# Top-k attention followed by a PReLU MLP: where a unit's first sign, k's copy, the weight preparation and the first loads of v stand

## The chip, the cores and the metric

The kernel runs on one core of a Trainium2 chip. The metric is the device time of one execution in microseconds (us). TensorE is called PE here, its weight loads PEld, VectorE DVE, ScalarE ACT, GpSimd POOL and SyncE SP. Each engine takes its own instructions in order; engines wait for each other through semaphores. A transfer (DMA) is issued from the instruction queue of SP, ACT or POOL and then runs on 16 shared DMA engines.

## The reference

64 heads (8 batches of 8) of 576 rows and 64 columns go through attention that keeps the 32 largest scores of each row; the heads of a batch are put side by side (4608 rows of 512), and a two-layer MLP with a PReLU between follows.

```python
scores = scale * np.matmul(q, k.transpose(0, 1, 3, 2))
kth = np.partition(scores, -32, axis=-1)[..., -32:-31]
scores = np.where(scores >= kth, scores, -1000000000.0)
attn = softmax(scores)
x = np.matmul(attn, v)            # then (b, s, h*d)
h = x @ w_in
g = np.maximum(h, 0.0) + alpha * np.minimum(h, 0.0)
out = g @ w_out
```

## The kernel before

**Tiles, units, pairs.** Two heads make a pair; a pair is cut into nine tiles of 128 rows by 576 scores (the ninth takes the last 64 rows of both heads). There are 32 pairs and 288 tiles. A program loop walks over the tiles; one turn is called a tick. Two tiles in a row make a unit (`unit_of`), the ninth tile of a pair a unit of one, so that a pair is 2+2+2+2+1. Every instruction is recorded in the order in which this loop names it, engine by engine: nothing is reordered later.

**One tile.** PE forms the scores (`scores`, L327, into `ps`). ACT copies them with a per-row shift into `b` (`act_b`, L336), takes their signs into `h` with a count per row (`act_s`, L342, the count is read out by a second instruction), and their exponentials into `e` (`act_e`, L347, once a unit). POOL turns the count into a flip word `SG` (`side_of`, L352). DVE flips the tile into `y` (L358), takes the largest eight of five strides (L369), merges them (L383, L385), picks the limit, and masks (`mk`, L432) a tile that is seven ticks old. POOL multiplies mask and exponentials into `w` (L442), SP transposes `w` by a DMA into `wT` (L455), PE multiplies with v (`av`, L493, into `pu`), DVE takes the reciprocal of the row sums (`rz`, L510), ACT scales into `xb` (L522).

**ACT's order in a unit.** In a unit's first tick ACT stands in this order: evacuations of the MLP step of the tick before, `b`, `b`, what the calendar of that tick holds, the sign of the first tile. In the second tick: evacuations of the first tick's MLP step, the sign of the second tile, the calendar, `e`.

**Preparing a pair.** `prep_plan` lists steps with ticks relative to a pair's base: transposes of q (`pe_q`, L196), copy of q (`act_q`, L199) and transposes of k (`pe_k`, L207), copy of k (`act_k`, L211) and transposes of the last 64 rows (`pe_t`, L215), their copy, then moments: `GK` (L228), `pr` (L237), `P` (`dve_p`, L245), `st`, and a short chain on DVE (L270 `sq` to L287) that gives the shift `NT` for `b`. `pq`, `pk`, `pt` share one PSUM bank, so each waits for the copy of the one ahead of it. `act_v` (L202) casts v from a float32 stage into `v_bf`.

**The MLP.** `mlp_steps` gives steps, one taken per tick from the queue `back`: 4 matmuls into `ph` (L696), evacuated by ACT with Relu into `gT` (L702), or 6 to 7 matmuls into `pz` (L710, L714), evacuated into `o_sb` (L719). A step's evacuation is run at the start of the next tick (queue `after`). In the main part there is one PSUM bank for it (`ps_m`), so a step's first matmul waits for the evacuation of the step before.

**Weights.** The first 48 ticks take steps of `weight_steps` instead: load alpha, load `w_out` in 16 blocks through three stage buffers, scale each twice on ACT (L643 by 1-alpha into `w_out_b`, L644 by alpha into `xT`, which is still free), load `w_in` with a cast from POOL (L631, two transfers for each of four blocks, at ticks 3, 7, 11, 15), transpose each block whole by a DMA from SP (L635, `w_inT`), and multiply (`w_id`).

Of the kernel before, what the change touches and what calls it, by code (L numbers as in the profile page):

```python
# [9 lines left out]
FP32 = mybir.dt.float32  # L10
# [6 lines left out]
S = 576  # L17
# [14 lines left out]
def kernel(  # L32
# [83 lines left out]
    def early_sets():  # L116
        for i in range(2):
            nc.gpsimd.memset(ksts[i][:, :, 0:1], 1.0)
            nc.gpsimd.memset(ksts[i][:, :, 129:130], 1.0)
            nc.gpsimd.memset(ksts[i][64:128, 4, :], 0.0)  # L120
        for t_ in st_vs:
            nc.vector.memset(t_[64:128, 4, :], 0.0)
            nc.vector.memset(t_[0:64, 5, :], 0.0)
        for t_ in v_bfs:
            nc.vector.memset(t_[:, :, D:V1], 1.0)
            nc.vector.memset(t_[64:128, 4, D:V1], 0.0)
            nc.vector.memset(t_[0:64, 5, D:V1], 0.0)
        for i in range(KW):
            nc.vector.memset(iota[:, i:i + 1], (1.0 + 2 * i) ** 2)

# [14 lines left out]

    def load_v(p):
        hA = 2 * p
        st_v = st_vs[p % 2]
        nc.sync.dma_start(st_v[:, 0:4, :], vf[hA, 0:512, :].rearrange("(c p) d -> p c d", p=128))
        nc.sync.dma_start(st_v[0:64, 4, :], vf[hA, 512:S, :])  # L150
        nc.sync.dma_start(st_v[64:128, 5, :], vf[hA + 1, 0:64, :])
        nc.sync.dma_start(st_v[:, 6:10, :],
                          vf[hA + 1, 64:S, :].rearrange("(c p) d -> p c d", p=128))

    ORDER = [divmod(n, TPP) for n in range(N0)]
    LAST = range(P0, NPAIR)
# [17 lines left out]
    def prep_plan(p):  # L174
# [33 lines left out]
                                    ident_f)  # L208

        def act_k():  # L210
            nc.scalar.copy(d["qkT"][:, 1, 0:512], d["pk"])  # L211

        def pe_t():
            d["pt"] = bank("pt", [128, 2, 64])
# [73 lines left out]
                                    ALU.bitwise_xor, ALU.bitwise_or)  # L288

        if p == 1:  # L290
            ts = [-9, -8, -7, -6, -5, -4, -3, -2, -2, -2, -2, -2, -1, -1, 1]
# [3 lines left out]
        steps = [dict(pe=[pe_q]), dict(act=[act_q], pe=[pe_k]), dict(act=[act_k], pe=[pe_t]),  # L295
                 dict(act=[act_t], pe=[pe_g]), dict(act=[act_g], pe=[pe_r]),
                 dict(dve=[dve_p]), dict(pe=[pe_s]), dict(act=[act_m]), dict(dve=[dve_2]),
                 {dvx: [dve_3]}, dict(dve=[dve_4]), {dvx: [dve_4b]}, dict(dve=[dve_5]),
                 dict(dve=[dve_6]), dict(act=[act_v])]
        if p == 0:  # L300
            ts = [-16, -15, -14, -13, -12] + [-11] * 6 + [-2]
            steps = [dict(pe=[pe_q, pe_g, pe_t]), dict(act=[act_q, act_g, act_t], pe=[pe_r, pe_k]),
                     dict(dve=[dve_p]), dict(act=[act_k], pe=[pe_s]), dict(act=[act_m])] + steps[8:]
        return list(zip(ts, steps))

    tiles = {}
# [33 lines left out]
    def act_s(n):  # L340
        h = attn.tile([128, S], BF16, name="h", bufs=1)
        nc.scalar.activation(h, tiles[n]["b"], AF.Sign, accum_out=S_all[:, n:n + 1])  # L342
# [250 lines left out]
    def last_pz():  # L593
        o0 = t7 + 384
        for h, (pool, tag) in enumerate(((ps_a, "pa"), (ps_m, "misc"))):
# [9 lines left out]
            (nc.scalar.copy if h == 0 else nc.vector.tensor_copy)(o_sb[:, 0:256], pz)  # L605
            nc.sync.dma_start(out[o0:o0 + 128, cs], o_sb[:, 0:256])

    def weight_steps():
        hold = {}

        def alpha():
            a16 = mlp.tile([128, DM], FP32, name="a16", tag="stage", bufs=3)[0:NFT, 0:128]
            nc.sync.dma_start(a16, moe_alpha.rearrange("(t p) -> t p", p=128))
            hold["a16"] = a16

        def alpha1():
            aps = ps_m.tile([128, NFT], FP32, name="aps", tag="misc")
            nc.tensor.transpose(aps, hold["a16"], ident_f[0:NFT, 0:NFT])
            hold["aps"] = aps
            hold["inT"] = mlp.tile([128, NKT, NFT, 128], BF16, name="w_inT", tag="gT", bufs=1)  # L620

        def alpha2():
            nc.scalar.copy(alpha_sb, hold["aps"])
            nc.gpsimd.tensor_scalar(alpha1m, alpha_sb, -1.0, 1.0, ALU.mult, ALU.add)

        def lin(f):
            return xT[:, f // 4, DM * (f % 4):DM * (f % 4 + 1)]

        def w_in(kk):
            for hf in range(0, DFF, 1024):  # L630
                nc.gpsimd.dma_start(w_in_b[:, kk, hf:hf + 1024],  # L631
                                    moe_w_in[kk * 128:(kk + 1) * 128, hf:hf + 1024])

        def w_in2(kk):
            nc.sync.dma_start_transpose(hold["inT"][:, kk, :, :], w_in_b[:, kk, :])  # L635

        def w_out(f):
            hold[f] = mlp.tile([128, DM], FP32, name="w_stage2", tag="stage", bufs=3)
            nc.sync.dma_start(hold[f], moe_w_out[f * 128:(f + 1) * 128, :])

        def w_out2(f):
            ws = hold.pop(f)
            nc.scalar.activation(w_out_b[:, f, :], ws, AF.Copy, scale=alpha1m[:, f:f + 1])  # L643
            nc.scalar.activation(lin(f), ws, AF.Copy, scale=alpha_sb[:, f:f + 1])  # L644

        done = [0]

        def w_id(kk, lim):
            if done[0] == 0:
                hold["pl", kk] = ps_m.tile([128, DM], FP32, name="pl", tag="misc")  # L650
            for f in range(done[0], lim):
                nc.tensor.matmul(hold["pl", kk], hold["inT"][:, kk, f, :], lin(f),
                                 start=(f == 0), stop=(f == NFT - 1))
            done[0] = lim % NFT

        def w_id2(kk):
            nc.scalar.copy(w_id_b[:, kk, :], hold["pl", kk])

        yield alpha, None
        yield (lambda: None), None  # L660
        yield (lambda: (alpha1(), w_out(0), w_out(1))), alpha2
        for f in range(NFT):
            yield ((lambda f=f: (w_out(f + 2) if f + 2 < NFT else None,
                                 w_in(f // 2) if f < 8 and f % 2 == 0 else None)),
                   (lambda f=f: w_out2(f)))
            yield ((lambda f=f: w_id(0, min(done[0] + 2, f)) if f >= 6 else None),
                   (lambda f=f: w_in2(f // 2) if f < 8 and f % 2 == 1 else None))
        yield (lambda: w_id(0, NFT)), (lambda: w_id2(0))
        for kk in range(1, NKT):
            for lim in (4, 8, 12, 16):  # L670
# [78 lines left out]
    with tc.manual_schedule(engines={E.PE, E.Activation, E.DVE, E.Pool, E.SP}):  # L749
# [66 lines left out]

        load(0, nc.scalar)
        load(1)
        plan(0)
        plan(1)  # L820
        early_sets()
        load_v(0)
        load_v(1)
        for t in range(-16, 0):
            for eng in ("act", "pool", "pe", "dve"):
                run(t, eng)
# [7 lines left out]
        n = 0  # L834
        end = max(NT + 24, 0)
        while n < end or back or after:
            for p in range(2, NPAIR):
                if n == max(0, BASE[p] - 18):
                    load(p)
                    plan(p)  # L840
                if n == max(0, BASE[p] - 13):
                    load_v(p)
# [5 lines left out]
            if n < NT:  # L848
                n0, m, i = unit_of[n]
                if i == 0:  # L850
                    act_b(n0)
                    if m == 2:
                        run(n, "act")
                    act_s(n)
                    if m == 1:
                        run(n, "act")
                        act_e(n0)
                else:
                    act_s(n)
                    run(n, "act")  # L860
                    act_e(n0)
# [6 lines left out]
            while back and credit > 0.0 and (first or nb == 2):  # L868
# [195 lines left out]
```

## Time and profile before

| | |
|---|---|
| Median of three runs | 873.18 us (868.11, 873.18, 873.46) |
| Profiled execution | 871.45 us; span of its instructions 869.6 us |
| PE busy | 714.7 us (82%) |
| POOL busy | 431.1 us (50%) |
| Mean granted clock of TensorE | 0.928 |
| Moved by DMA | 99.34 MB, mean 114 GB/s |

The page gives busy time by engine, the span in 40 slices, the chain of waits that ended last, and groups of equal instructions with the idle time ahead of them and what ended it. The span is 1.85 us shorter than the execution's own time. A tick lasts some 2.7 us, a pair some 25.

### The profile page before, as it was taken

To read this page: it belongs to the slowest core of one execution; us is meant where nothing else is said; L and a number is where in the kernel's file an instruction comes from. 1 tells how busy PE (TensorE), PEld (TensorE's weight loads), DVE (VectorE), ACT (ScalarE), POOL (GpSimd) and SP (SyncE) were. 2 spreads that over 40 slices of the span, in tenths; PEclk is the share of its full clock that TensorE was granted. 3 is DMA by queue.
4 is the path that set the end of the run, shared out by engine and by line. 5 is a ranking of instruction groups with operands and counts; after the bars stand their busy time and mean duration, and the time that the engine had idled before them with its cause. 6 is when DMAs were issued, how large, how long until landed. Compare 5 with 4: busy or idle time off the path is not lost. (4 is left out here: it accounts for less than half of the span.)

```text
span 869.6 us, 20320 instructions
## 1 busy us (share of the span) xinstructions
PE 714.7 (82%) x5697; PEld 424.1 (49%) x5771; DVE 814.2 (94%) x4900; ACT 789.5 (91%) x1873; POOL 431.1 (50%) x630
## 2 busy tenths in 40 slices
PE   6666778778977789877987789987897988899996
PEld 4333444434544445544454445643455554566575
DVE  4988999999999999999999999998999999988992
ACT  6989999989999999998999989999999899979871
POOL 1454555555455555554554555554555555545530
PEclk8567789899999999999998999989999999999999
DMA  7799645554675645464477556564365644535452
GB/s 159 157 159 209 128 92 102 121 94 88 134 153 111 105 108 124 99 134 88 110 159 121 88 104 119 118 132 97 84 125 123 124 100 85 100 74 100 89 99 56
DMA packets 342616, 99.34 MB, mean 114 GB/s; under 512 B 334672, under 2 KB 334944, under 8 KB 342496
## 3 DMA queue, kind: packets, MB, share of 16 engines
q1 hardware_dynamic: 340144, 95.58, 56.0%
q0 software_dynamic: 1152, 2.10, 1.8%
q8 instruction: 47, 0.77, 0.4%
q14 instruction: 73, 0.60, 0.2%
q10 hardware_dynamic: 1200, 0.30, 0.2%
HBM read 36.71 MB, written 9.44 MB: 53 GB/s over the span
## 5 line engine op out<-in xcount | busy, mean ns | idle before, releaser
L442 POOL TENSOR_TENSOR w<-mk,e 128x576 bf16<-128x576 bf16 x250 | 319.1, 1277 | 333.1 <-DVE mk L432 186.3
L369 DVE MAX8 C<-y 128x8 f32<-128x112 f32 (+1 forms) x1440 | 380.0, 264 | 0.1
L327 PE MATMUL ps<-qkT 64*128 64x288 f32 (+1 forms) x1280 | 252.8, 467 | 36.9 <-ACT b L336 36.5
L336 ACT ACTIVATE b<-ps,NT 128x576 f32<-128x576 f32 x288 | 202.4, 761 | 5.7 <-PE ps L327 5.7
L342 ACT ACTIVATE h<-b 128x576 bf16<-128x576 f32 x288 | 202.9, 705 | 1.6
L696 PE MATMUL ph<-xT,w_in_b 128*128 128x128 bf16 (+2 forms) x997 | 151.2, 293 | 41.6 <-ACT gT L702 38.4
L327 PEld LDWEIGHTS ps<-qkT 64*128 64x128 f32 (+1 forms) x1280 | 131.2, 190 | 97.7 <-ACT b L336 60.8
L347 ACT ACTIVATE e<-b 128x1152 bf16<-128x1152 f32 (+1 forms) x158 | 174.3, 1103 | 0.0
L358 DVE TENSOR_SCALAR y<-b,SG 128x576 int32<-128x576 int32 x288 | 147.4, 512 | 11.2 <-POOL SG L352 8.6
L383 DVE MAX8 L<-C 128x8 f32<-128x40 f32 x864 | 155.7, 180 | 0.1
L432 DVE TENSOR_SCALAR mk<-b,KP 128x576 bf16<-128x576 f32 x282 | 143.8, 510 | 0.0
L714 PE MATMUL pz<-w_out_b,gT 128*128 128x512 bf16 x543 | 132.4, 380 | 1.2 <-issue 0.5
L696 PEld LDWEIGHTS <-w_in_b 128*128 128x128 bf16 x1024 | 80.9, 100 | 105.8 <-issue 81.6
L702 ACT ACTIVATE gT<-ph 128x512 bf16<-128x512 f32 x140 | 85.9, 621 | 26.4 <-PE ph L696 26.2
L385 DVE MATCH_REPLACE8 C<-L,C 128x40 f32<-128x40 f32 x576 | 103.8, 180 | 0.0
L714 PEld LDWEIGHTS <-gT 128*128 128x128 bf16 x560 | 51.6, 98 | 68.5 <-issue 14.0
L493 PE MATMUL pu<-v_bf,wT 128*128 128x65 bf16 (+1 forms) x1600 | 69.1, 198 | 12.3 <-DMA wT<-w 11.1
L352 POOL TENSOR_SCALAR SG<-S_all 128x1 int32<-128x1 f32 x288 | 65.2, 227 | 22.0 <-ACT h L342 21.8
L493 PEld LDWEIGHTS <-wT 128*128 128x128 bf16 (+1 forms) x1600 | 64.9, 103 | 22.3 <-DMA wT<-w 11.7
L442 POOL TENSOR_TENSOR wm<-mk,e 128x576 bf16<-128x576 bf16 x32 | 40.9, 1277 | 49.0 <-DVE mk L432 46.4
L342 ACT ACTIVATION_READ_ACCUMULATOR h<-b 128x1 f32 x288 | 62.8, 218 | 0.0
L522 ACT ACTIVATE xb<-pu,rz 128x64 bf16<-128x64 f32 x224 | 54.6, 371 | 0.0
(113 smaller groups left out, 724.1 us busy)
## 6 DMA issues: line engine op xcount, KB each, us to landing
out_dram<-o_sb SPq DMA_DIRECT2D x34, 256.0 KB, 2.3
st_q<-in_q_dram SPq DMA_DIRECT2D x64, 128.0 KB, 2.8
st_v<-in_v_dram SPq DMA_DIRECT2D x64, 128.0 KB, 2.6
kst<-in_k_dram SPq DMA_DIRECT2D x62, 128.0 KB, 2.7
w_stage<-in_moe_w_out_dram SPq DMA_DIRECT2D x16, 256.0 KB, 3.3
w_in_b<-in_moe_w_in_dram POOLq DMA_DIRECT2D x8, 256.0 KB, 6.7
wT<-w SPq DMA_TRANSPOSE x128, 3.3
st_q<-in_q_dram SPq DMA_DIRECT2D x32, 32.0 KB, 2.5
```

The source lines that it names most:

```text
L327: nc.tensor.matmul(o_, l_, r_, start=True, stop=True)
L336: nc.scalar.activation(t["b"].rearrange("p (a c) -> p a c", a=2), t["ps"], AF.Identity, bias=NT0[:, p * TPP + j:p * TPP + j + 1], scale=ON ...
L342: nc.scalar.activation(h, tiles[n]["b"], AF.Sign, accum_out=S_all[:, n:n + 1])
L347: nc.scalar.activation(e, tiles[n0]["bu"], AF.Exp, scale=scl)
L358: nc.vector.tensor_scalar(t["y"].bitcast(I32), t["b"].bitcast(I32), FLIP, SG[:, n:n + 1], ALU.bitwise_xor, ALU.bitwise_xor)
L369: return [lambda g=g: nc.vector.max(out=C[:, n % TPP, g, :], in_=y[:, g:S // 8:NSEG, :]) for g in range(NSEG)]
L383: ops.append(lambda r=r, src=src: nc.vector.max(out=L[:, 8 * r:8 * r + 8], in_=src))
L432: nc.vector.tensor_scalar(t["mk"], t["b"], row_limit(n), None, ALU.is_ge)
L442: nc.gpsimd.tensor_tensor(dst, t["mk"], t["e"], ALU.mult)
L493: nc.tensor.matmul(o_, wT[:, 4 * side + c, cs], d["v"][:, 5 * side + c, :], start=(c == 0), stop=(c == 4))
L696: nc.tensor.matmul(hold[f][:, i, :], w_in_b[:, kk, (f + i) * 128:(f + i + 1) * 128], xT[:, kk, c0:c0 + tb], start=(kk == 0), stop=(kk == N ...
L714: nc.tensor.matmul(pz[0:m], hold["gT"][:, f, r0:r0 + m], w_out_b[:, f, :], start=False, stop=(f == NFT - 1))
```

## The change

- **Signs.** In a unit of two, both signs now stand in the second tick, behind the evacuations of the first tick's MLP step. Units of one keep their order.
- **k's copy.** `act_k` moves from the calendar of the next unit (behind its two `b`) to a new slot `actz` at the very end of the tick of `pe_k`, behind `e`. For pair 0 it goes to DVE.
- **v of pairs 0 and 1.** Loaded by casting transfers from POOL's queue straight into `v_bf`, with no stage and no `act_v`: pair 0 at the start, pair 1 one part at the end of each of ticks 8 to 11. The pad rows of all `v_bf` are now zeroed over their whole width by DVE.
- **Weights.** alpha is loaded right behind the loads of pairs 0 and 1. The five first scalings by 1-alpha go to POOL, one per tick in ticks 2 to 6, with the one by alpha on ACT; the other eleven blocks take one scaling per tick with a free tick behind most of them. The casts of `w_in` are issued at ticks 3, 11, 19, 27, and each transposition is cut into four, two ticks apart. The last three `w_id` take three steps instead of four. In all 49 steps instead of 48.

```diff
-            nc.vector.memset(t_[64:128, 4, D:V1], 0.0)
-            nc.vector.memset(t_[0:64, 5, D:V1], 0.0)
+            nc.vector.memset(t_[64:128, 4, :], 0.0)
+            nc.vector.memset(t_[0:64, 5, :], 0.0)
...
+    def load_v(p, parts=range(4)):
...
+        dst = v_bfs[p][:, :, 0:D] if p < 2 else st_vs[p % 2]
+        en = nc.gpsimd if p < 2 else nc.sync
...
+        for i in parts:
+            en.dma_start(*moves[i])
...
         def act_k():
-            nc.scalar.copy(d["qkT"][:, 1, 0:512], d["pk"])
+            (nc.vector.tensor_copy if p == 0 else nc.scalar.copy)(d["qkT"][:, 1, 0:512], d["pk"])
...
-        steps = [dict(pe=[pe_q]), dict(act=[act_q], pe=[pe_k]), dict(act=[act_k], pe=[pe_t]),
+        steps = [dict(pe=[pe_q]), dict(act=[act_q], pe=[pe_k], actz=[act_k]), dict(pe=[pe_t]),
...
-        def w_in2(kk):
-            nc.sync.dma_start_transpose(hold["inT"][:, kk, :, :], w_in_b[:, kk, :])
+        def w_in2(kk, i):
+            nc.sync.dma_start_transpose(wh["inT"][:, kk, 4 * i:4 * i + 4, :],
+                                        w_in_b[:, kk, 512 * i:512 * i + 512])
...
+        def scale(f, one_m, pool=False):
+            dst, s = (w_out_b[:, f, :], alpha1m) if one_m else (lin(f), alpha_sb)
+            if pool:
+                nc.gpsimd.tensor_scalar(dst, wh[f], s[:, f:f + 1], None, ALU.mult)
+            else:
+                nc.scalar.activation(dst, wh[f], AF.Copy, scale=s[:, f:f + 1])
...
+        ins = {3 + 8 * kk: (lambda kk=kk: w_in(kk)) for kk in range(NKT)}
+        more = {7 + 8 * kk + 2 * i: (lambda kk=kk, i=i: w_in2(kk, i))
+                for kk in range(NKT) for i in range(4)}
...
+        for f in range(5):
+            yield ((lambda f=f, k_=k_: (w_out(f + 2), scale(f, True, True), put_in(k_))),
+                   (lambda f=f: scale(f, False)))
+            k_ += 1
+        for f in range(5, NFT):
+            yield ((lambda f=f, k_=k_: (w_out(f + 2), put_in(k_))),
+                   (lambda f=f: scale(f, True)))
+            yield ((lambda f=f, k_=k_: (w_id(0, min(done[0] + 2, f) if k_ > 12 else 0),
+                                        put_in(k_ + 1))),
+                   (lambda f=f: scale(f, False)))
+            k_ += 2
+            if f % 6 != 4:
+                yield (lambda k_=k_: put_in(k_)), None
+                k_ += 1
...
+            if 8 <= n < 12:
+                put(n, "end", lambda i=n - 8: load_v(1, [i]))
...
                     act_b(n0)
                     if m == 2:
                         run(n, "act")
-                    act_s(n)
-                    if m == 1:
+                    else:
+                        act_s(n)
                         run(n, "act")
                         act_e(n0)
                 else:
+                    act_s(n0)
                     act_s(n)
...
             run(n, "pe")
+            run(n, "actz")
```

More of the change, by code (lines that the diff above doesn't have):

```diff
@@ L606, in last_pz, with load_alpha @@
             nc.sync.dma_start(out[o0:o0 + 128, cs], o_sb[:, 0:256])
-    def weight_steps():
[L609 to L614, printed above, removed]
+    wh = {}
+    def load_alpha():
+        a16 = mlp.tile([128, DM], FP32, name="a16", tag="stage", bufs=3)[0:NFT, 0:128]
+        nc.sync.dma_start(a16, moe_alpha.rearrange("(t p) -> t p", p=128))
+        wh["a16"] = a16
+    def weight_steps():
         def alpha1():
             aps = ps_m.tile([128, NFT], FP32, name="aps", tag="misc")
-            nc.tensor.transpose(aps, hold["a16"], ident_f[0:NFT, 0:NFT])
-            hold["aps"] = aps
-            hold["inT"] = mlp.tile([128, NKT, NFT, 128], BF16, name="w_inT", tag="gT", bufs=1)
+            nc.tensor.transpose(aps, wh["a16"], ident_f[0:NFT, 0:NFT])
+            wh["aps"] = aps
+            wh["inT"] = mlp.tile([128, NKT, NFT, 128], BF16, name="w_inT", tag="gT", bufs=1)
         def alpha2():
-            nc.scalar.copy(alpha_sb, hold["aps"])
+            nc.scalar.copy(alpha_sb, wh["aps"])
             nc.gpsimd.tensor_scalar(alpha1m, alpha_sb, -1.0, 1.0, ALU.mult, ALU.add)
@@ L632, in w_in @@
                                     moe_w_in[kk * 128:(kk + 1) * 128, hf:hf + 1024])
-        def w_in2(kk):
-            nc.sync.dma_start_transpose(hold["inT"][:, kk, :, :], w_in_b[:, kk, :])
+        def w_in2(kk, i):
+            nc.sync.dma_start_transpose(wh["inT"][:, kk, 4 * i:4 * i + 4, :],
+                                        w_in_b[:, kk, 512 * i:512 * i + 512])
         def w_out(f):
[L638 to L644, printed above, removed]
+            if f < NFT:
+                wh[f] = mlp.tile([128, DM], FP32, name="w_stage2", tag="stage", bufs=3)
+                nc.sync.dma_start(wh[f], moe_w_out[f * 128:(f + 1) * 128, :])
+        def scale(f, one_m, pool=False):
[4 more added lines that the diff above has]
+                nc.scalar.activation(dst, wh[f], AF.Copy, scale=s[:, f:f + 1])
         done = [0]
         def w_id(kk, lim):
-            if done[0] == 0:
-                hold["pl", kk] = ps_m.tile([128, DM], FP32, name="pl", tag="misc")
+            lim = max(lim, done[0])
+            if done[0] == 0 and lim > 0:
+                wh["pl", kk] = ps_m.tile([128, DM], FP32, name="pl", tag="misc")
             for f in range(done[0], lim):
-                nc.tensor.matmul(hold["pl", kk], hold["inT"][:, kk, f, :], lin(f),
+                nc.tensor.matmul(wh["pl", kk], wh["inT"][:, kk, f, :], lin(f),
                                  start=(f == 0), stop=(f == NFT - 1))
@@ L656, in w_id2, with put_in @@
         def w_id2(kk):
-            nc.scalar.copy(w_id_b[:, kk, :], hold["pl", kk])
-        yield alpha, None
-        yield (lambda: None), None
[L661 to L667, printed above, removed]
+            nc.scalar.copy(w_id_b[:, kk, :], wh["pl", kk])
+        ins = {3 + 8 * kk: (lambda kk=kk: w_in(kk)) for kk in range(NKT)}
+        more = {7 + 8 * kk + 2 * i: (lambda kk=kk, i=i: w_in2(kk, i))
+                for kk in range(NKT) for i in range(4)}
+        def put_in(k_):
+            ins.get(k_, int)()
+            more.get(k_, int)()
+        yield (lambda: (alpha1(), w_out(0), w_out(1))), alpha2
+        yield (lambda: None), None
+        k_ = 2
+        for f in range(5):
[12 more added lines that the diff above has]
+                k_ += 1
         yield (lambda: w_id(0, NFT)), (lambda: w_id2(0))
         for kk in range(1, NKT):
-            for lim in (4, 8, 12, 16):
+            for lim in (6, 11, 16):
                 yield ((lambda kk=kk, lim=lim: w_id(kk, lim)),
@@ L818 @@
         load(1)
+        load_alpha()
         plan(0)
@@ L822 @@
         load_v(0)
-        load_v(1)
         for t in range(-16, 0):
```

19 lines of the change are left out of this document (9 added, 10 removed).

## The prediction

> **What bounds the kernel now.** I read the page's busy times first, then DVE's waits, then the stretches, then single units on the timeline.
>
> ```profile
> span 869.6 us, 20320 instructions
> ...
> PE 714.7 (82%) x5697; PEld 424.1 (49%) x5771; DVE 814.2 (94%) x4900; ACT 789.5 (91%) x1873; POOL 431.1 (50%) x630
> ```
>
> Two engines are nearly full. 871.45 us is the profiled execution's own time, 1.85 us of it outside the span.
>
> ```profile
> DVE P L245 <- PE pr L237: 12.0, 12, 2.3
> DVE y L358 <- POOL SG L352: 8.6, 7, 3.5
> DVE rz L510 <- PE pu L493: 5.5, 4, 2.8
> DVE sq L270 <- ACT M L266: 2.0, 2, 1.0
> ```
>
> These are DVE's waits that this change can reach: engine, line, what it waited for, us in total, times, longest. Together 28.1 us; the rest of DVE's idle time is the start and the end.
>
> ```profile
> 40.00:60.00 20.00, 10.85 (x66) 7.06 (x63) 17.63 (x109) 17.02 (x37) 12.38 (x19) 0.59 1.10 155
> ...
> 500.00:600.00 100.00, 86.75 (x690) 49.79 (x700) 98.03 (x591) 93.20 (x228) 52.59 (x75) 0.96 0.59 115
> ```
>
> Columns: length, then PE, PEld, DVE, ACT and POOL busy, granted clock, DMA share, GB/s. In mid-kernel DVE is busy 98.03 of 100 us, so nothing there can be worth more than 2%. In the front it is 17.63 of 20 while the DMA share is 1.10 and the clock 0.59: that is where idle time stands and where most of the edits are.
>
> **The signs (steady part).** A unit of two whose first tick has an MLP evacuation looks like this:
>
> ```profile
> 377.08 1.28 POOL L442 TENSOR_TENSOR w<-mk,e 128x576 bf16<-128x576 bf16 x1 [1.12 <-issue]
> 377.33 1.39 ACT L336 ACTIVATE b<-ps,NT 128x576 f32<-128x576 f32 x2
> 377.51 1.02 PE L696 MATMUL ph<-xT,w_in_b 128*128 128x512 bf16 x4 [0.72 <-ACT gT L702]
> ...
> 378.58 0.71 ACT L342 ACTIVATE h<-b 128x576 bf16<-128x576 f32 x1
> ...
> 379.15 0.23 ACT L342 ACTIVATION_READ_ACCUMULATOR h<-b 128x1 f32 x1
> 379.25 0.63 ACT L702 ACTIVATE gT<-ph 128x512 bf16<-128x512 f32 x1
> 379.72 0.72 ACT L342 ACTIVATE h<-b 128x576 bf16<-128x576 f32 x1
> ...
> 381.08 0.23 POOL L352 TENSOR_SCALAR SG<-S_all 128x1 int32<-128x1 f32 x1
> 381.43 0.51 DVE L358 TENSOR_SCALAR y<-b,SG 128x576 int32<-128x576 int32 x1
> ```
>
> The change puts gT ahead of the first h. PE's last ph matmul ends at 378.53 (377.51 + 1.02) and the second b at 378.72, so ACT need not wait for PE: the room is 0.19 us. gT comes 0.67 us sooner (379.25 - 378.58), the first sign 0.47 later (379.72 - 379.25). ACT's total is unchanged. y started 2.05 us after the sign's count was out (381.43 - 379.38), so here DVE feels nothing. PE gets its bank sooner, but in units like this the PE is not what DVE or ACT waits for. Cost here: nothing, covered by those 2.05 us. Without this cover:
>
> ```profile
> 592.66 0.25 ACT L342 ACTIVATION_READ_ACCUMULATOR h<-b 128x1 f32 x1
> 592.99 0.23 POOL L352 TENSOR_SCALAR SG<-S_all 128x1 int32<-128x1 f32 x1
> 593.29 0.51 DVE L358 TENSOR_SCALAR y<-b,SG 128x576 int32<-128x576 int32 x1
> ```
>
> Here y follows the count by 0.38 us, nearly all of it SG, and the sign's 0.47 us would be seen in full. But a unit like this is one in which ACT is late anyway, and DVE pays for that a few ticks on:
>
> ```profile
> 395.61 1.88 PE L327 MATMUL ps<-qkT 64*128 64x288 f32 x6 [1.73 <-ACT b L336]
> ...
> 399.79 0.82 DVE L245 TENSOR_TENSOR P<-pr,qkT 128x512 bf16<-128x512 f32 x2 [2.00 <-PE pr L237]
> ```
>
> PE's scores wait for ACT's b of the single tile, MLP and pr queue behind them, DVE's P waits 2.00 us. What DVE loses at y it no longer loses at P, whose time ACT and PE set. So I put the signs at 0, with +0.5 for units in which PE is too late for the earlier gT; bounds -2 and +5 (ten or so units at 0.47).
>
> **k's copy.**
>
> ```profile
> PEld pt L215 <- ACT qkT L211: 34.5, 26, 2.6
> L207 PE MATMUL pk<-ident_f,kst 128*128 128x128 f32 x128 | 22.2, 300 | 7.8 <-ACT qkT L199 7.0
> 380.56 1.23 ACT L347 ACTIVATE e<-b 128x1152 bf16<-128x1152 f32 x1
> ```
>
> PE's 34.5 us go, but they are idle time of an engine that ends no wait of DVE there: 0. ACT does the same copy one unit earlier, behind e. pk's four matmuls (4 x 0.27 to 0.30, about 1.1 us) run during e's 1.23 us, so ACT does not wait for them. If PE is late, each of 31 pairs could cost a few tenths: -1 to +3, taken as 0.
>
> **The transposes.** This is the largest term.
>
> ```profile
> 40.78 1.90 SPq L455 DMA_TRANSPOSE wT<-w  x1
> 40.89 1.27 POOL L631 DMA_DIRECT2D w_in_b<-in_moe_w_in_dram  x2
> 42.79 9.98 SPq L635 DMA_TRANSPOSE w_inT<-w_in_b  x1
> 53.94 0.18 DVE L510 RECIPROCAL rz<-pu 128x4 f32<-128x4 f32 x1 [2.16 <-PE pu L493]
> 82.19 0.18 DVE L510 RECIPROCAL rz<-pu 128x4 f32<-128x4 f32 x1 [2.75 <-PE pu L493]
> DMA to landing us min/median/max: 2.6/4.0/12.3
> ```
>
> One whole w_inT kept SP's queue for 9.98 us; every wT behind it was late, and the wT issued at 40.78 landed after 12.3 us, beside two casts of w_in. PE waited for it, then DVE: 2.16 us, and 2.75 a second time. Afterwards a w_inT piece is a quarter, and the third and fourth casts come eight ticks apart. The wT of tick 10 still meets a cast at tick 11, so I do not give it all: -4.0 of 4.9; bounds -4.9 and 0. The Trainium skill, "DMA: Bandwidth & Descriptors", section "Queues, rings and completion order", says an engine serves its queues in turn, a whole packet each. By that rule the wT stays behind the cast however small the w_inT pieces are, and only the second stall would go: the sum would be 2 us higher.
>
> **The start and POOL.**
>
> ```profile
> 10.93 0.73 ACT L202 CAST v_bf<-st_v 128x640 bf16<-128x640 f32 x1 [1.63 <-DMA st_v<-in_v_dram]
> ...
> 11.56 1.37 ACT L336 ACTIVATE b<-ps,NT 128x576 f32<-128x576 f32 x2
> ...
> 18.14 0.21 ACT L342 ACTIVATION_READ_ACCUMULATOR h<-b 128x1 f32 x1
> 18.64 1.30 POOL L631 DMA_DIRECT2D w_in_b<-in_moe_w_in_dram  x2
> 19.97 0.44 POOL L352 TENSOR_SCALAR SG<-S_all 128x1 int32<-128x1 f32 x2
> 20.25 0.52 DVE L358 TENSOR_SCALAR y<-b,SG 128x576 int32<-128x576 int32 x1 [2.58 <-POOL SG L352]
> ```
>
> The first b stood behind the cast of v: up to 0.63 us come back (11.56 - 10.93), or up to as much is lost because v's casting loads now run beside the first loads of q and k; -0.35. The third sign was counted at 18.35 but its SG stood behind w_in's issue until 19.97: 1.6 us. The issue stays in tick 3 but POOL reaches it sooner; k's copy now delays that sign by some 0.6: -0.8. In ticks 4 to 7 one scaling by alpha stands ahead of the signs instead of behind e, 0.73 us each, and the second wait of sq for M (1.0) grows with it: +1.4. First nine ticks: -0.35 - 0.8 + 1.4 = +0.25; bounds -1.5 and +2.
>
> New on POOL: five scalings of 128x512 in ticks 2 to 6, when it has only SG. The trace has none; between one 128x1 SG (0.23) and one 128x576 w (1.28), nearest w, so about 1 us, and DVE has about 1.5 us between y and y then: 0. The four parts of v for pair 1 at the ends of ticks 8 to 11 sit between SG and w, where POOL was idle 1.12 us. A cast piece of w_in takes 0.65 (1.30 / 2); a large part of v has 512 runs against 128, so 0.65 to 2.6. SG is queued behind w, y waits for SG, all of DVE behind y. Two large parts cost 0 to 1.5 each, the small one together with w_in at tick 11 (0.65 + 1.27 against 1.12) about 0.8: 0 to +3.8, taken +1.3.
>
> **ACT's relief.**
>
> ```profile
> L643 ACT ACTIVATE w_out_b<-w_stage,alpha1m 128x512 bf16<-128x512 f32 x16 | 11.7, 729 | 0.0
> L202 ACT CAST v_bf<-st_v 128x640 bf16<-128x640 f32 x32 | 23.3, 730 | 1.6 <-DMA st_v<-in_v_dram 1.6
> ```
>
> Five scalings and two casts leave ACT: 7 x 0.73 = 5.1 us. P's waits (12.0 us) are where an earlier ACT shows, but ACT runs ahead of DVE by a few buffers only, and cannot keep more lead than they hold. -2.0; bounds 0 and -10.
>
> **The sum.** +0.25 (first ticks) +1.3 (POOL) -4.0 (transposes) -2.0 (ACT's relief) +0.5 (late units) = -3.95. Against the profiled execution 871.45 - 3.95 = 867.5; the median of the runs lies 1.7 higher, so by it 869.2. I forecast 868. Some 1% (8.7 us) is what a measurement of this kernel can tell from no change, so by itself this is within 1%.
>
> **Rivals.**
>
> *ACT was the true bound (27%).* If ACT's 5.1 us and the stall of the transposes pass through whole, most of P's waits go too: -4.9 - 8 (two thirds of 12.0) + 1.55 (first ticks and POOL) = -11.4, 860. For it: P's 12 waits go back to ACT's b. Against it: the 2.05 us of cover at 381 show ACT ahead of DVE.
>
> *POOL becomes the queue that DVE stands behind (15%), the slower side.* POOL's chain w, SG, y leaves 1.12 us of room a tick. If a scaling takes w's 1.28 and falls between two y, and each part of v takes 2.6, then 5 x 0.6 over what DVE covers, 4 x 1.5 for v, and 5 for the signs of late units come to +14, less 2 left of the transposes' gain: 883. It decides from the point at which a POOL addition outlasts 1.12 us. The Trainium skill, "SBUF — State Buffer", section "SBUF: two separate sides", has a rule for it: while DVE runs in a two-port mode, POOL cannot write descriptors, and a transfer of 0.62 us is stretched to 3.1. This trace does not agree: the pair of casts at 40.89 beside DVE's work took 1.27 us, the one at 18.64 took 1.30.
>
> *The edits shift the stalls but remove none (10%).* The cast at tick 11 still delays wT, and DVE waits as before: 871 to 874.
>
> **Numbers.** The forecast has 48%; 3 of these reach a gain over 1%. Faster by over 1%: 27 + 3 = 30%. Slower by over 1%: 15%. Within 1%: 45 + 10 = 55%. The range 857 to 877 takes in the faster rival, the unchanged one and the bounds of the forecast, and leaves out most of the slower rival and a little at the low end.
>
> **What would show it.** rz's two waits below 1 us in total, and w_inT issues of one to two us, would confirm the transposes; a wT still landing after over 10 us, the skill's rule on packets. gT ahead of the first h with less than 0.2 us of wait would confirm the signs; y waiting for SG in many units would refute them. PE's wait of pt for k's copy should be gone with the span hardly moved by it. POOL's v issues over 1.2 us, with y idle behind SG in ticks 9 to 12, would be the slower rival. P's waits below 5 us in total would be the faster one. I am wrong if mid-kernel DVE time per tick changes at all.

## The result, and the profile after

| | before | after |
|---|---|---|
| Median of the runs | 870.8 us (868.11 to 873.46, 6 runs) | 902.49 us (900.23 to 906.24, 6 runs) |
| Profiled execution | 871.45 us | 900.23 us |
| Span | 869.6 us | 898.5 us |
| Mean granted clock of TensorE | 0.928 | 0.900 |

The changed kernel takes 1.038 times as long (95% interval 1.0346 to 1.0414). The page of the changed kernel, span and busy times:

```profile
span 898.5 us, 20312 instructions
...
PE 734.8 (82%) x5696; PEld 431.6 (48%) x5771; DVE 818.6 (91%) x4901; ACT 798.3 (89%) x1865; POOL 445.0 (50%) x643
```

ACT runs eight instructions fewer than before (1865 against 1873) and is busy 8.8 us longer (798.3 against 789.5). That is the first thing to explain. DVE's busy time grew by 4.4 us, so most of the 28.9 us of span is DVE standing still. Its waits in the changed kernel (engine, line, what it waited for, us in total, times, longest):

```profile
DVE P L247 <- PE pr L239: 28.9, 22, 3.6
DVE y L362 <- POOL SG L356: 19.3, 31, 2.6
...
DVE sq L272 <- ACT M L268: 3.0, 1, 3.0
...
DVE rz L514 <- PE pu L497: 1.4, 2, 1.0
```

Against the waits of before, P grew from 12.0 to 28.9 us, y from 8.6 to 19.3 (7 times to 31), and sq from 2.0 to 3.0; rz fell from 5.5 to 1.4. Only the last two went the way that the prediction forecast. The stretches of the changed kernel (length, PE, PEld, DVE, ACT, POOL busy, clock, DMA share, GB/s):

```profile
500.00:600.00 100.00, 83.23 (x639) 46.72 (x646) 93.88 (x571) 92.28 (x225) 50.95 (x72) 0.95 0.52 104
```

The loss is in the steady part. DVE was busy 98.03 of these 100 us before and is busy 93.88 now. The starts of y show the same: y of tile 54 (counted from 0) stands 0.4 us earlier than before, y of tile 108 10.4 later, of tile 180 18.8, of the last tile 27.2. About 1 us is lost in each pair of heads.

One unit of the changed kernel on the timeline (start, duration, engine, line; idle time and its releaser in brackets):

```profile
397.77 0.61 ACT L727 ACTIVATE gT<-ph 128x512 bf16<-128x512 f32 x1
...
398.25 0.71 ACT L346 ACTIVATE h<-b 128x576 bf16<-128x576 f32 x1
...
398.82 0.23 ACT L346 ACTIVATION_READ_ACCUMULATOR h<-b 128x1 f32 x1
399.09 0.68 ACT L346 ACTIVATE h<-b 128x576 bf16<-128x576 f32 x1
399.14 0.22 POOL L356 TENSOR_SCALAR SG<-S_all 128x1 int32<-128x1 f32 x1 [0.86 <-ACT h L346]
399.40 0.52 DVE L362 TENSOR_SCALAR y<-b,SG 128x576 int32<-128x576 int32 x1 [0.66 <-POOL SG L356]
```

gT stands ahead of the signs, as the change says. Two readings matter. The second sign starts 0.84 us behind the first (399.09 - 398.25), where before a sign was followed by gT after 0.67 and gT by a sign after 0.47. And y follows SG at once, with DVE idle 0.66 us: the cover of 2.05 us that the prediction quoted is gone here.

### The profile page after: what moved, and what is told of

The parts are those of the page before. It is cut to its first block, busy times and chain, and to the rows that moved or that the text cites. A ratio compares the mean times of both kernels' runs of the same rounds, so it can differ in the third digit from the quotient of the medians.

```text
span 898.5 us, 20312 instructions
## 1 busy us (share of the span) xinstructions
PE 734.8 (82%) x5696; PEld 431.6 (48%) x5771; DVE 818.6 (91%) x4901; ACT 798.3 (89%) x1865; POOL 445.0 (50%) x643
## 5 line engine op out<-in xcount | busy, mean ns | idle before, releaser
L331 PE MATMUL ps<-qkT 64*128 64x288 f32 (+1 forms) x1280 | 262.0, 482 | 54.5 <-ACT b L340 53.9
L346 ACT ACTIVATE h<-b 128x576 bf16<-128x576 f32 x288 | 198.1, 688 | 5.0
L340 ACT ACTIVATE b<-ps,NT 128x576 f32<-128x576 f32 x288 | 200.3, 746 | 2.0 <-PE ps L331 2.0
L331 PEld LDWEIGHTS ps<-qkT 64*128 64x128 f32 (+1 forms) x1280 | 135.9, 197 | 118.4 <-ACT b L340 78.5
L351 ACT ACTIVATE e<-b 128x1152 bf16<-128x1152 f32 (+1 forms) x158 | 170.7, 1080 | 0.0
L362 DVE TENSOR_SCALAR y<-b,SG 128x576 int32<-128x576 int32 x288 | 148.6, 516 | 21.4 <-POOL SG L356 19.3
L739 PE MATMUL pz<-w_out_b,gT 128*128 128x512 bf16 x542 | 135.0, 385 | 1.2 <-issue 0.5
L727 ACT ACTIVATE gT<-ph 128x512 bf16<-128x512 f32 x140 | 83.0, 600 | 22.6 <-PE ph L721 21.7
L346 ACT ACTIVATION_READ_ACCUMULATOR h<-b 128x1 f32 x288 | 56.8, 197 | 0.0
L744 ACT COPY o_sb<-pz 128x512 f32<-128x512 f32 x35 | 20.7, 593 | 36.1 <-PE pz L739 36.1
```

The costliest lines, as they stand in the source:

```text
L331: nc.tensor.matmul(o_, l_, r_, start=True, stop=True)
L340: nc.scalar.activation(t["b"].rearrange("p (a c) -> p a c", a=2), t["ps"], AF.Identity, bias=NT0[:, p * TPP + j:p * TPP + j + 1], scale=ON ...
L351: nc.scalar.activation(e, tiles[n0]["bu"], AF.Exp, scale=scl)
L362: nc.vector.tensor_scalar(t["y"].bitcast(I32), t["b"].bitcast(I32), FLIP, SG[:, n:n + 1], ALU.bitwise_xor, ALU.bitwise_xor)
L739: nc.tensor.matmul(pz[0:m], hold["gT"][:, f, r0:r0 + m], w_out_b[:, f, :], start=False, stop=(f == NFT - 1))
```

## The experiments

Three theories were set against each other. **S**: the moved signs cost it. **K**: k's copy at the end of the tick costs it. **F**: the front (weights, loads of v) costs it. Every kernel was compared with the kernel before on its own chip, and the ratios below are against that.

### Which part costs

k's copy back:

```diff
-        steps = [dict(pe=[pe_q]), dict(act=[act_q], pe=[pe_k], actz=[act_k]), dict(pe=[pe_t]),
+        steps = [dict(pe=[pe_q]), dict(act=[act_q], pe=[pe_k]), dict(act=[act_k], pe=[pe_t]),
```

> The changed kernel with k's copy where it stood before (behind the two b of the next unit); the signs stay behind the evacuation. Theory K: the changed kernel loses its 30 us because ACT, in order, waits at the end of the tick for PE's four pk transposes, which stand behind an MLP step in PE's queue: then this kernel is at 870 to 875. Theory S: the moved signs cost it (y follows the sign's count without cover): then it stays above 892. Theory F: the weight preparation and the loads of v cost it: it stays at 900 to 904.

Measured: 885.01 us, ratio 1.0152 (1.0102 to 1.0202).

Signs back:

```diff
                     if m == 2:
                         run(n, "act")
-                    else:
-                        act_s(n)
+                    act_s(n)
+                    if m == 1:
                         run(n, "act")
                         act_e(n0)
                 else:
-                    act_s(n0)
                     act_s(n)
```

> The changed kernel with the first sign back in the unit's first tick; k's copy stays at the end of the tick. Theory K: stays above 892, with ACT's waits for pk still there. Theory S: 870 to 876, with y no longer waiting for SG in the middle of the kernel. Theory F: 900 to 904. If both K and S hold, each of the first two kernels takes back a part and the two parts add up to about 30 us.

Measured: 884.57 us, ratio 1.0142 (1.0084 to 1.0199).

Both edits together:

> The changed kernel with both back: only the loads of v, the scalings, the casts of w_in and the quartered transposes differ from the kernel before. Theories K and S: 866 to 872, since the first tiles of the changed kernel are level with those of the kernel before up to about 156 us (0.4 us ahead at tile 48). Theory F: 895 to 904.

Measured: 867.64 us, ratio 0.9976 (0.9949 to 1.0002).

F falls: the front alone costs nothing. S and K both hold. Above the front alone the signs are worth 1.8% (1.0152 - 0.9976) and k's copy 1.7%, some 15 us each. Together with the front's -0.2% that makes 3.2% of the 3.8%; the rest is within the intervals of the four ratios, so that it needs both edits is not shown. The granted clock is lower in the slower kernels (0.900 in the changed one against 0.928), but does not carry the loss: at 0.911 the front alone took 870.07 us and the kernel with the signs back 886.18, and the changed kernel at 0.913 took 900.99.

### What the signs cost

```diff
-    NV = 6
+    NV = 5
...
-        h = attn.tile([128, S], BF16, name="h", bufs=1)
+        h = attn.tile([128, S], BF16, name="h", bufs=2)
```

With five buffers, v of the later pairs is overwritten before the second half of their rows has used it.

> The changed kernel with a second buffer for the sign's output h (and five instead of six v_bf, to make room). Two signs that follow each other directly start 0.82 us apart, where a sign and an evacuation start 0.67 and 0.47 us apart. Theory H, a part of S: the pitch comes from both signs writing the same buffer; with two buffers it falls to 0.6 to 0.7 and some 0.15 us in each of about 128 units comes back, 10 to 20 us: 883 to 892. If the pitch belongs to the sign with its count, nothing changes: 900 to 904, and the pitch stays at 0.82.

Measured: 887.74 us, ratio 1.0198 (1.0154 to 1.0241). The next kernel keeps all six v buffers, takes the room from the bf16 identity, and has k's copy back:

```diff
-    ident_b = const.tile([128, 128], BF16, name="ident_b")
-    nc.gpsimd.tensor_copy(ident_b, ident_f)
+    ident_b = ident_f.bitcast(BF16).rearrange("p (n h) -> p n h", h=2)[:, :, 1]
```

> The changed kernel with k's copy back in the next unit and two buffers for h (room for it: the bf16 identity becomes a strided view of the float32 one); the signs stay behind the evacuation. With one buffer it took 885.0. Theory H: the 130 direct pairs of signs at 0.81 instead of 0.67 us are all that the moved signs cost (130 x 0.14 = 18 us of ACT): 866 to 870, level with the front alone (867.6). Rival: y's lost cover behind the later first sign is a price of its own: 873 to 880.

Measured: 869.54 us, ratio 1.0015 (0.9986 to 1.0044), against 1.0152 with one buffer. A unit of this kernel on ACT's timeline:

```profile
388.08 0.65 ACT L726 ACTIVATE gT<-ph 128x512 bf16<-128x512 f32 x1
388.55 0.74 ACT L345 ACTIVATE h<-b 128x576 bf16<-128x576 f32 x1
389.13 0.26 ACT L345 ACTIVATION_READ_ACCUMULATOR h<-b 128x1 f32 x1
389.22 0.74 ACT L345 ACTIVATE h<-b 128x576 bf16<-128x576 f32 x1
```

The same order, and the second sign now starts 0.67 us behind the first, while the first one's count is still being read out; with one buffer it started behind that (399.09 against 398.82 + 0.23). Over all 130 units of two, the median pitch of sign to sign is 0.82 us in the changed kernel and 0.67 with two buffers, so one buffer costs 130 x 0.15 = 19 us of ACT. ACT's busy time says much the same. The first line is of the changed kernel with k's copy back (one buffer):

```profile
PE 733.9 (83%) x5771; PEld 428.4 (48%) x5771; DVE 818.7 (92%) x4901; ACT 798.3 (90%) x1865; POOL 445.3 (50%) x643
```

and this one of the same kernel with two buffers (and the strided identity):

```profile
PE 724.3 (84%) x5771; PEld 427.2 (49%) x5771; DVE 818.0 (94%) x4901; ACT 782.6 (90%) x1865; POOL 444.0 (51%) x642
```

The same 1865 instructions on ACT, 15.7 us less. So theory H holds. For the rival (y's lost cover as a price of its own) some 0.4% remain between 1.0015 and 0.9976, whose intervals overlap.

The front alone with two buffers (and the strided identity):

> The front alone (signs and k's copy as before the change) with two buffers for h and the strided identity. There a sign never stands directly behind a sign, so by theory H nothing is to be had: 866 to 869. If instead any second buffer helps ACT (the sign waits for its buffer also across other work): 855 to 862. It also shows that the strided identity costs nothing.

Measured: 865.83 us, ratio 0.9971 (0.9947 to 0.9995). The expectation was not quite right: a sign stands directly behind a sign here too, in 22 of the 130 units, where nothing falls between them. Their pitch falls from 0.82 to 0.67 us, 3 us of ACT in all, and the second buffer brings nothing that can be told from none (867.64 without it).

### What k's copy costs

With the signs back, ACT's waits have a group that the front alone hardly has (0.7 us there):

```profile
ACT qkT L213 <- PE pk L209: 18.1, 11, 5.8
```

One of them, in the same kernel, first on ACT and then on PE:

```profile
236.24 1.21 ACT L351 ACTIVATE e<-b 128x1152 bf16<-128x1152 f32 x1
238.30 0.59 ACT L213 COPY qkT<-pk 128x512 f32<-128x512 f32 x1 [0.85 <-PE pk L209]
```

```profile
236.14 1.04 PE L735 MATMUL pz<-w_id_b,xT 128*128 128x512 bf16 x4
237.01 0.81 PE L739 MATMUL pz<-w_out_b,gT 128*128 128x512 bf16 x3
237.66 0.60 PE L209 MATMUL pk<-ident_f,kst 128*128 128x128 f32 x4
```

The matmuls of the tick's MLP step run while e runs, and pk comes behind them. ACT is idle 0.85 us, with the next unit's evacuation, both b and all that follows queued behind the copy. Six of the eleven waits are of this kind, 4.8 us together. In the other five, 13.3 us, scores or matmuls of the weights stand ahead of pk. The longest is in the front, on PE and then on ACT:

```profile
53.49 0.73 PE L497 MATMUL pu<-v_bf,wT 128*128 128x65 bf16 x10 [5.19 <-DMA wT<-w]
...
56.38 1.04 PE L661 MATMUL pl<-xT,w_inT 128*128 128x512 bf16 x2
57.20 1.06 PE L209 MATMUL pk<-ident_f,kst 128*128 128x128 f32 x4
58.30 0.59 ACT L213 COPY qkT<-pk 128x512 f32<-128x512 f32 x1 [5.83 <-PE pk L209]
```

PE itself stood 5.19 us for a wT, with pk behind it in its queue. So part of this price falls in the front: y of tile 54, ahead of the first of those six waits, is 6.7 us later than in the front alone, and y of the last tile 19.8.

To tell the wait from the mere place of the copy, pk was made ready earlier, with the copy left where it is. First by one tick:

```diff
+        if p > 1 and p not in (LEAD1, LEAD2):
+            ts = [-15, -14, -13] + ts[2:]
+            steps = [dict(pe=[pe_q]), dict(act=[act_q], pe=[pe_k]), dict(actz=[act_k])] + steps[2:]
```

> The changed kernel with the signs back in the first tick (884.6, ACT idle 17 us longer than in the front alone, 18.2 us of its waits for pk), and with pq, q's copy and pk one tick earlier for pairs from 2 on (but two: 11 and 20); k's copy stays at the end of the same tick. Theory K (ACT waits there for pk, which stands behind the MLP step): the waits of qkT for pk fall below 3 us and the time to 867 to 872. Rival, the place: 0.47 us of copy ahead of the next unit's evacuation and b delays PE's scores whether pk is ready or not: 878 to 886 with the waits gone.

Measured: 894.73 us, ratio 1.0303 (1.0273 to 1.0334): slower still, and neither expectation. The wait of qkT for pk is gone, but PE has a new one:

```profile
PE pk L209 <- ACT qkT L201: 45.3, 30, 4.2
```

It was 8.4 us in the kernel with the signs back. The tick earlier is the first of a unit, where q's copy stands behind the two b; now PE stands still for it, with the next scores and the MLP behind. The edit moved q's copy along with pk, so the next one goes two ticks early, where q's copy is in a unit's second tick again:

```diff
+            ts = [-16, -15, -13] + ts[2:]
...
-                if n == max(0, BASE[p] - 18):
+                if n == max(0, BASE[p] - 19):
```

> As the kernel with pk a tick early, but pq, q's copy and pk two ticks early (and the pair's loads one), so that q's copy stands in a unit's second tick again, where pk found it done before; k's copy at the end of the same tick as in the change, signs in the first tick. It is to be set against 884.6 (pk in the same tick). The tick-early kernel lost at another place (PE waited 45 us for q's copy behind the two b). Theory K (ACT's wait for pk is the price): waits of qkT for pk under 3 us, PE's wait for q's copy under 12, time 867 to 873. Rival, the place of the copy ahead of the next evacuation and b: 877 to 886 with those waits gone. Half and half: 873 to 877.

Measured: 864.4 us, ratio 0.9907 (0.9889 to 0.9925), against 1.0142. The copy stands where the change put it, and ACT no longer waits for it:

```profile
560.32 1.15 ACT L354 ACTIVATE e<-b 128x1152 bf16<-128x1152 f32 x1
561.37 0.56 ACT L213 COPY qkT<-pk 128x512 f32<-128x512 f32 x1
561.84 0.59 ACT L747 COPY o_sb<-pz 128x512 f32<-128x512 f32 x1
```

So theory K holds: the wait is the price, and the place shows none. The time is below the expectation, and below the front alone (0.9976). What the earlier loads, pq and q's copy bring by themselves was not tried.

pk ahead of the MLP step in PE's queue, in the same tick (signs back):

```diff
-dict(act=[act_q], pe=[pe_k], actz=[act_k])
+dict(act=[act_q], pe0=[pe_k], actz=[act_k])
...
+            run(n, "pe0")
             nb = 1 if n < N0 + 2 else 2
```

> The changed kernel with the signs back (884.6) and pk's transposes ahead of the tick's MLP step in PE's queue instead of behind it. Theory K says that ACT's wait comes from the MLP step in front of pk: the waits of qkT for pk fall from 18 to under 5 us; but PE now waits for q's copy with the MLP step behind it. If that is covered: 868 to 873; if it moves the stall to the MLP step: 876 to 890 with more wait of pk for q's copy (8.4 us now) and of gT and o_sb.

Measured: 876.68 us, ratio 1.0066 (1.0048 to 1.0085). ACT's waits for pk fell from 18.1 to 9.4 us, and PE's wait for q's copy rose from 8.4 to 26.1. The longest wait left, 4.7 us, is again in the front. About half of the price is still there, now partly on PE: not every wait came from the MLP step.

### Both mended at once

The whole change with two buffers for h, and pk one tick early:

> The whole change with both prices taken away: two buffers for h, and pq, q's copy and pk one tick earlier. If H and K are all that it lost: 864 to 870. If the two orders cost something besides: 873 to 882.

Measured: 903.29 us, ratio 1.038 (1.0338 to 1.0422); pk stood one tick early here, with the stall just shown, so this decides nothing. With pk two ticks early:

> The whole change (signs behind the evacuation, k's copy at the tick's end, new front) with two buffers for h and with pq, q's copy and pk two ticks early. If H (sign behind sign in one buffer) and K (ACT's wait for pk) are all that the change lost: 862 to 869, 35 us below the changed kernel. If the two orders together cost something besides: 873 to 885.

Measured: 876.61 us, ratio 1.0097 (1.006 to 1.0133). Of the 3.8% loss 2.8 points are gone and 1.0 is left, as the second expectation had it. DVE's waits in this kernel:

```profile
DVE y L364 <- POOL SG L358: 14.7, 16, 3.5
DVE P L246 <- PE pr L238: 10.9, 10, 2.8
```

and in the one with the signs back and pk two ticks early:

```profile
DVE P L247 <- PE pr L239: 11.8, 14, 2.3
DVE y L365 <- POOL SG L359: 8.3, 12, 3.8
```

P is back at the 12.0 us of before; y is not. The 6.4 us more at y are of the size of the two spans' difference, 5.6 us (872.3 - 866.7). That fits signs standing behind evacuations: ACT's wait of o_sb for PE is 35.6 us there and 27.7 here, and with the first sign behind it, the sign waits too. This last link is read from the totals and was not tried by itself, and the medians differ by more than the spans (12 us).

### Terms of the front

Each transposition of w_in whole again, where its first quarter was (front alone):

```diff
-        more = {7 + 8 * kk + 2 * i: (lambda kk=kk, i=i: w_in2(kk, i))
-                for kk in range(NKT) for i in range(4)}
+        more = {7 + 8 * kk: (lambda kk=kk: nc.sync.dma_start_transpose(
+            wh["inT"][:, kk, :, :], w_in_b[:, kk, :])) for kk in range(NKT)}
```

> The front alone (867.6) with each transposition of w_in whole again, issued where its first quarter was. The prediction put the quartered transposes at -4.0 us. If so: 870 to 873, with rz's waits for pu back at 2 us or more in the front. If the casts' new distance of eight ticks did it and not the quarters: 866 to 869.

Measured: 862.88 us, ratio 0.9914 (0.9892 to 0.9936): faster than the front alone with quarters, and below both expectations. SP's queue in this kernel:

```profile
31.09 3.20 SPq L669 DMA_TRANSPOSE w_inT<-w_in_b  x1
...
53.71 2.14 SPq L669 DMA_TRANSPOSE w_inT<-w_in_b  x1
```

Before, one whole transposition held the queue for 9.98 us, issued 1.9 us behind a cast of w_in; here the four whole ones take 2.11 to 3.20, each issued over 11 us behind a cast. So it was not the quarters that freed the queue; what fits is the casts' distance of eight ticks, which was not tried by itself. Whole, the transpositions hold the queue for 10 us in all, in quarters for about 20 (16 of 1.28), and PE's waits for wT are 5.4 us with whole ones and 10.3 with quarters. Up to tile 54 the gain over the quarters is 0.9 us; it grows to 5.0 by the last tile, where the instructions are the same. Why it grows stays open; P's waits are 7.5 us against 13.1.

The five scalings back on ACT (front alone):

```diff
-                yield ((lambda f=f, k_=k_: (w_out(f + 2), scale(f, True, True), put_in(k_))),
+                yield ((lambda f=f, k_=k_: (w_out(f + 2), scale(f, True), put_in(k_))),
```

> The front alone (867.6) with the five scalings on POOL back on ACT, in the same ticks behind e. The prediction put ACT's relief (5.1 us of work, 3.65 of it these five) at -2.0 us. If so: 868.5 to 870. If ACT's work in the first ticks passes whole: 871 to 872. If POOL's scalings cost something (y behind SG): below 867.

Measured: 870.07 us, ratio 0.9989 (0.9966 to 1.0011). That lies between the first two expectations, and the interval overlaps that of the front alone. By tile 18, y is 3.6 us later than there, which is the whole of 5 x 0.73; by the last tile 2.5.

### Towards a better kernel

Signs back, pk two ticks early, whole transposes:

> Signs in the first tick, pq, q's copy and pk two ticks early, k's copy at the tick's end (864.4 so far), with whole transposes of w_in, which took the front alone from 867.6 to 862.9. If the two gains add up: 858 to 861. If P's waits were only shifted by them: 862 to 865.

Measured: 866.25 us, ratio 0.997 (0.9936 to 1.0004): above both expectations; the two gains do not add up. Whole transposes made this kernel slower (0.997 against 0.9907) where they made the front alone faster, so what grew there behind tile 54 can't be put down to them.

The whole change, both mended, whole transposes:

> The whole change with both mended (two buffers for h, pk two ticks early) and whole transposes. If the signs behind the evacuation bring anything at last (PE gets its bank 0.67 us sooner): 853 to 858. If not: as with the signs in the first tick, 858 to 863.

Measured: 876.05 us, ratio 1.0082 (1.0051 to 1.0114): as without them, so a miss for both expectations, and once more the moved signs and k's copy cost something together.

The front alone, whole transposes, two buffers for h:

> The front alone with whole transposes (862.9) and two buffers for h. The second buffer brought the front alone 1.8 us at most (865.8 against 867.6, intervals overlapping); here 861 to 863, or 858 to 861 if it is real.

Measured: 861.9 us, ratio 0.9916 (0.9884 to 0.9948). Within its interval this is the same as the front alone with whole transposes (0.9914). Either is 0.8 to 0.9% faster than the kernel before, with the new front, whole transposes, and the orders of ACT as they were. So is the kernel with the signs back and pk two ticks early (0.9907).

## Why the prediction was wrong

**Signs, put at 0.** The step that failed is "ACT's total is unchanged". No instruction was added, but with the signs moved ACT is busy 14.5 us longer (798.3 us with k's copy back, against 783.8 in the front alone), since in all 130 units of two the signs now follow each other and both write the one buffer h. In the order of before, another operation stood between them in 106 units; in the other 24 sign followed sign, 0.83 us apart (median). One of them, in the kernel before:

```profile
431.74 0.69 ACT L342 ACTIVATE h<-b 128x576 bf16<-128x576 f32 x1
432.32 0.21 ACT L342 ACTIVATION_READ_ACCUMULATOR h<-b 128x1 f32 x1
...
432.56 0.68 ACT L342 ACTIVATE h<-b 128x576 bf16<-128x576 f32 x1
```

The pitch is 0.82 us, while an evacuation starts 0.67 behind a sign. The size of the price could have been read there: 106 x 0.15 = 16 us. The Trainium skill, "Perfetto Trace Analysis", section "Optimizing Scalar/DVE Operations", says that an operation's latency in the profile is about twice its access overhead because the write's acknowledgement overlaps the next instruction, and gives about 93 ns for ScalarE on SBUF. This case shows 0.15 us between one buffer and two; whether that is such an overlap lost, or a wait that the program sets for the buffer, no run here tells apart.

The second part of the step, y's cover of 2.05 us, held only while ACT was ahead. With ACT late, y waited for SG 31 times. The prediction had named that as what would refute it, and had put late units at +0.5; with both causes mended some 1% is still left, and its cause stays open. The room of 0.19 us was read too wide: ACT starts an instruction before the one ahead has ended (378.58 against 378.72), so it was 0.05. That did not decide: ACT's waits for ph and pz were 51.5 us before, and 54.4 with the signs moved and k's copy back.

**k's copy, put at 0.** The step that failed is "pk's four matmuls run during e's 1.23 us, so ACT does not wait for them". In PE's queue they stand behind what that tick gave PE first, the MLP step or scores or matmuls of the weights, and that is what runs during e. The upper bound of 3 us came from "a few tenths" for late pairs; the waits came to 12.3 us in the whole change and 18.1 in the kernel with the signs back, up to 5.8 each, and the time to 1.7%. That PE's idle time at pt was worth nothing did hold: in the kernel with the signs back PEld waits 10.1 us there instead of 34.5, and the time is longer.

**Transposes, put at -4.0, and ACT's relief, put at -2.0.** Between tiles 12 and 36, y of the front alone moves from 0.6 us behind the kernel before to 5.4 ahead, 6.0 us, the sum of both. rz's waits fell to 0.2 us. The reason given was wrong, though: whole transpositions with the casts apart do no worse than quarters. And PE's stall, from which DVE's was to come, hardly shrank: in the front alone PE waits 10.3 us for wT against 11.1 before, only earlier (until 50.7 and 76.1 us instead of 53.2 and 81.4). The wT beside the cast of tick 11 still landed late; the view of wT in the changed kernel between 40 and 56 us:

```profile
L459 SPq DMA_TRANSPOSE wT<-w x3: 1407/2017/2853, 43.4 to 55.1; - x3
...
DMA to landing us min/median/max: 3.6/6.2/8.3
```

The longest took 8.3 us, and PE waited 4.3 us for it. The prediction had named over 10 us as the sign of the Trainium skill's rule on packets, so the runs do not bear that rule out; the dearer sum worked out from it did not come either, since DVE hardly waited for that wT. Of the relief, the part tried (3.65 us on POOL) passes whole at first, 3.6 us by tile 18, but only 2.5 by the last tile, so -2.0 was not far off.

**First nine ticks, +0.25, and POOL, +1.3.** y of tile 8 stands 0.1 us behind the kernel before in the front alone. Between tiles 8 and 12 there are 0.5 us more. That +0.25 fits is partly luck: sq's second wait, which was to grow, is 3.0 us in the changed kernel and absent in the front alone. The scalings on POOL, put at 0 and about 1 us each, took 1.69. In the changed kernel y of tile 1 waited 1.22 us for an SG that stood behind a scaling, and in the front alone four y that start just behind a scaling take 0.83 to 0.95 us instead of 0.51. Back on ACT they cost more all the same. The parts of v on POOL, in the changed kernel:

```profile
35.47 0.83 POOL L155 DMA_DIRECT2D v_bf<-in_v_dram  x1
...
38.65 0.58 POOL L155 DMA_DIRECT2D v_bf<-in_v_dram  x1
...
42.04 0.70 POOL L155 DMA_DIRECT2D v_bf<-in_v_dram  x1
...
45.29 0.92 POOL L155 DMA_DIRECT2D v_bf<-in_v_dram  x1
```

The large ones take 0.83 and 0.92 us, near the lower bound of 0.65; none of POOL's times is stretched to 3.1, so the Trainium skill's rule that was weighed for the slower rival did not show here either. That rival lost its ground: in the front of the changed kernel no y waited longer behind POOL's own work than those 1.22 us.

**The sum.** By its own terms the front was right: -4.45 forecast, -4.8 at the last tile in the front alone, 0.9976 in the ratio. That its parts fit is in some measure luck, as said. (By six runs the median before is 870.8, 0.65 below the profiled execution and not 1.7 above it.) The loss came from the two terms set to nothing. Of the rivals, "ACT was the true bound" had half of it: ACT does set the pace, but the change gave it more to do instead of less. And the last sentence of the prediction, that it is wrong if DVE's time per tick changes in mid-kernel, is what happened.

## What to carry to other kernels

Moving an instruction changes the cost of its neighbours: look at what will stand directly ahead of it, and whether the two share a buffer. An edit at an engine's queue that moves a consumer forward needs the producer's whole queue in front of it, not only the producer's own duration. Two engines at 91 and 94% are both bounds: with the second buffer for h ACT was busy 15.7 us less, and the time fell by about as much (ratio 1.0152 to 1.0015).

## What the runs showed of the hardware

- Two ACT signs of 128x576 into the same buffer start 0.82 us apart (median of 130), into two buffers 0.67, though neither reads what the other writes.
- A DMA transposition of a 128x2048 block held SP's queue for 1.93 to 3.49 us in seven of eight cases (the kernel before, and the front alone with whole ones), and for 9.98 in the one issued 1.9 us behind a casting transfer; that the cast is the cause was not tried.
- Four y of 128x576 on DVE that started 0.05 to 0.16 us behind a POOL scaling took 0.83 to 0.95 us (front alone); two that started 0.02 and 0.55 us behind one took the usual 0.51 (changed kernel).
- On POOL a scaling of 128x512 by a column, float32 to bf16, takes 1.69 us, over twice ACT's 0.73, and more than the 128x576 product of two bf16 tiles (1.28):

```profile
L650 POOL TENSOR_SCALAR w_out_b<-w_stage,alpha1m 128x512 bf16<-128x512 f32 x5 | 8.4, 1688 | 1.6 <-DMA w_stage<-in_moe_w_out_dram 1.6
```
